# A fused LSH-attention and spatial-gating kernel: a wide hash product for the first pair, another order of the last batch's units, and per-batch priorities

## The chip, the cores and the metric

The kernel runs on one core of a Trainium2 chip. The metric is the device time of one execution in microseconds (us), lower is better. In the profile the engines are PE (TensorE's products), PEld (its weight loads), DVE (VectorE), ACT (ScalarE), POOL (GpSimd) and SP (SyncE, which issues all the transfers here).

## The reference, cut to what matters

Attention with 8 heads of width 64 over 4 batches of 768 rows, in which a query sees only the keys whose six sign bits (a hash by a random projection) are the same as its own; its output goes through a gated unit whose gate mixes rows with a 768 x 768 matrix.

```python
q_bits, k_bits = (q @ proj > 0), (k @ proj > 0)          # 6 bits per row
mask = bucket(q_bits)[:, :, :, None] == bucket(k_bits)[:, :, None, :]
attn = softmax(np.where(mask, q @ k.T / 8, -1e9))         # (4, 8, 768, 768)
x = (attn @ v).transpose(0, 2, 1, 3).reshape(4, 768, 512)
h = np.maximum(x @ w_in, 0.0)                             # 512 -> 1024
u, vv = h[..., :512], h[..., 512:]
v_n = (vv - mean) / np.sqrt(var + 1e-06)
v_s = np.einsum('ts,bsd->btd', w_spatial, v_n) + b_spatial[None, :, None]
out = (u * v_s) @ w_out                                   # 512 -> 512
```

## The kernel before, in words

Two heads make a pair, so there are 16 pairs, four per batch. For each pair (`pair`, L318) one load brings 128 x 2 x 768 numbers of k and q (L323). A hash product in float32 (L325) gives 4 x 32 rows; VectorE takes the sign (L331), ScalarE scales it (L333), and the rows go through DRAM (a write, L338, two reads, L342) into `hr`, where they stand as 12 rows of 64 per head among rows of zeros. ScalarE and VectorE split k and q into a high and a low half in float16 (`hl`, L354 and L357), and v likewise (`vp`, L361 and L363).

A pair has six row blocks. For each (`scores`), TensorE makes the scores of two heads in 16 products, three of the halves and one of the hash rows per half row and head; VectorE cuts them at a floor and takes the row maximum (L403, L406), ScalarE makes the exponentials and their sums (L411), VectorE the reciprocals (L413, L414), ScalarE the high half of the weights (L417), VectorE the low half (L419), and a transfer transposes both (L425). After three blocks a weighted product (`weighted`, 36 products in two column halves) makes half of the pair's `xt` (L446, L449).

When a batch's four pairs are done, `mlp` runs its 28 units on TensorE: six v (normalised by L479 to L515, POOL makes the low half, L518), then for each half of the rows four u, four s (L555, L558, L564, L567 make the gated block `g` in two halves) and three o. The units of one batch run beside the attention of the next batch; those of the last batch run alone. The gated unit's weights are loaded and converted once, in pieces (`weights` and `job`): 16 of w_in and 8 of w_out go through one step on ScalarE (L295), three on VectorE (L299 to L303) and a split (L242, L313), 12 of w_sp through two copies on ScalarE (L308, L309) and L313.

The order of all instructions is set when the program is built. Every step is given an engine, a duration, a key and its buffers (`op`); `plan` runs through time with these durations and, whenever an engine is free, gives it the ready step with the smallest key, if a buffer of its ring is free (6 for ex, 4 for pp, 2 for the score buffers, 1 for qk). The result is each engine's fixed order, and SP's too. A key is counted in row blocks: `g = NT*p + i` for block i of pair p, `k0 = NT*(p - 1) + 0.4` for a pair's preparation. The units have keys from `NT*NPAIR*(b + 1) + 2` on, and each step its offset, the same for all batches. For instance:

```python
op("PE", 1.36, g - 12.0, product, r=[hl, hrb], w=ps, kind="s")
op("DVE", 0.88, g, cut, r=[ps[e]], w=[ex[e], mx])
op("DVE", 0.93, g + 3.0, lambda e=e: nc.vector.scalar_tensor_tensor(
UNITS = [("v", i, 0) for i in range(NT)] + [x for h in range(2) for x in
         [("u", d, h) for d in range(NF)] + [("s", d, h) for d in range(NF)] + [("o", h * NT // 2 + i, 0) for i in range(NT // 2)]]
```

Of the kernel before, what the change touches and what calls it, by code (L numbers as in the profile page):

```python
# [34 lines left out]
def lsh_attention_spatial_gating(  # L35
# [34 lines left out]


# [8 lines left out]
    ws = [const.tile([P, NT, S], F16, name=f"ws{i}") for i in range(2)]  # L80
    wo = [const.tile([P, NF, DM], F16, name=f"wo{i}") for i in range(2)]
# [50 lines left out]

    def plan():


        SEM, MODE, DMA_LAT, SLOW = 0.1, 0.1, 1.3, 1.25
# [11 lines left out]
        fed = False  # L148
# [35 lines left out]
        while done < len(ops):  # L184
            nxt = None
            for e in free:
                while free[e] <= now:
# [24 lines left out]
                    if e == "PE":  # L212
                        if not fed:
                            d *= SLOW
                        fed = fed or o.kind == "m"
# [47 lines left out]
    Wv, Wu, Ws, Wo, Bt = Buf(), Buf(), Buf(), Buf(), Buf()  # L263

    def weights():
        vi, vo, vs = (x.rearrange("(c p) f -> p c f", p=P) for x in (w_in, w_out, w_sp))
        n = 0
        for src, dst, cs, lo, hi, m, f, W, key, dk in (
                (vi, wi, NPAIR, F2, DF, 256, SI, Wv, 5.0, 1.9), (vi, wi, NPAIR, 0, F2, 256, SI, Wu, 20.5, 1.0),
                (vs, ws, NT, 0, S, HS, SW, Ws, 28.0, 0.5), (vo, wo, NF, 0, DM, 256, SI, Wo, 33.5, 0.5)):  # L270
            for c in range(cs):
                for h in range(lo, hi, m):
                    job(n, src[:, c, h:h + m], [w[:, c, h:h + m] for w in dst], m, f, W, key)
                    n += 1
                    key += dk
        op("SP", 0.6, 27.0, lambda: nc.sync.dma_start(out=bt, in_=b_sp.partition_broadcast(P)), w=[Bt], land=1.0)

    def job(n, src, dst, m, f, W, key):
# [5 lines left out]
        op("SP", 0.6, key - 1.5, fetch, w=[raw], land=0.85 if m == 256 else 1.05)  # L284
        if src.dtype == F32:
            wb = raw
        else:
# [17 lines left out]
            for k, e, d in ((0, "ACT", 0.33), (1, "DVE", 0.2), (2, "DVE", 0.34), (3, "DVE", 0.34)):  # L305
                op(e, d, key - 12.0, lambda k=k: conv(k), r=[raw], w=[wb], lock=e == "DVE")
        if src.dtype == F32:
            op("ACT", 0.41, key, lambda: nc.scalar.activation(dst[0], wb.t[:, :m], AF.Copy, scale=f), r=[wb], w=[(W, n)])  # L308
            op("ACT", 0.41, key, lambda: nc.scalar.activation(wb.t[:, :m], wb.t[:, :m], AF.Copy, scale=f), w=[wb])  # L309
        else:  # L310
            op("ACT", 0.31, key + 1.5, lambda eng: cast(eng, dst[0], wb.t[:, :m]), r=[wb], w=[(W, n)], alt=("DVE", 0.2))
        op("POOL", 0.63 if m == 256 else 0.87, key,
           lambda: nc.gpsimd.tensor_tensor(out=dst[1], in0=wb.t[:, :m], in1=dst[0], op=ALU.subtract), r=[wb], w=[(W, n)], lock=True)  # L313
# [5 lines left out]
    def pair(p):  # L319
        b, r = divmod(p, NPAIR)  # L320
        k0 = NT * (p - 1) + 0.4 if p else -40.0
        qk, v32, hl, vp, hrb, hp, s0, s1 = (Buf(t) for t in ("qk", "v32", "hl", "vp", "hr", "m", "sg0", "sg1"))
        op("SP", 0.6, k0 - 1.9, lambda: nc.sync.dma_start(out=tile_of(qk, wk, [P, 2, S], F32, f"qk{p}"), in_=kq[b, r]), w=[qk], land=2.4)  # L323

        def hash_():  # L325
            t = tile_of(hp, ps_m, [P, 512], F32, f"hp{p}")
            matmuls([(t[32 * j:32 * j + 32, :HS], pj, qk.t[:, j // 2, (j % 2) * HS:(j % 2 + 1) * HS],
                      True, True, (0, 32 * j)) for j in range(4)])
# [11 lines left out]
        def rows(e):  # L340
            hrb.t = hr[p % NHR]
            nc.sync.dma_start(  # L342
                out=hrb.t[D * e:D * e + NR].rearrange("r g (c k) -> r (g c) k", c=2),
                in_=d.t.rearrange("(j r) k -> r j k", j=4)[16 * e:16 * e + NR])

        for e in range(2):
            op("SP", 0.6, k0 + 0.3 + 3.7, lambda e=e: rows(e), r=[d], w=[(hrb, e)], land=0.3)

        def part(g):
            return hl.t.rearrange("p (x g) s -> p x g s", g=2)[:, :, g]  # L350

        def high():
            tile_of(hl, wk, [P, 4, S], F16, f"hl{p}")
            nc.scalar.activation(part(0), qk.t, AF.Copy, scale=SQ)  # L354
# [19 lines left out]
    def scores(p, i, hl, hrb, pts):  # L374
# [22 lines left out]
        op("PE", 1.36, g - 12.0, product, r=[hl, hrb], w=ps, kind="s")  # L397

        for e in range(2):
# [5 lines left out]
            op("DVE", 0.88, g, cut, r=[ps[e]], w=[ex[e], mx])  # L405
        op("DVE", 0.08, g, lambda: nc.vector.tensor_scalar(tile_of(nb, wk, [P, 2], F32, f"nb{p}_{i}"), mx.t, -ISQ, None, op0=ALU.mult), r=[mx], w=[nb])  # L406
        for e in range(2):
# [4 lines left out]
            op("ACT", 0.92, g + 0.7, exp, r=[nb], w=[ex[e], sm])  # L412
        op("DVE", 0.08, g, lambda: nc.vector.tensor_scalar(tile_of(ri, wk, [P, 2], F32, f"ri{p}_{i}"), sm.t, 1e-9, 1.0 / SP, op0=ALU.add, op1=ALU.mult), r=[sm], w=[ri])  # L413
        op("DVE", 0.1, g, lambda: nc.vector.reciprocal(ri.t, ri.t), w=[ri])  # L414
        j = i % 3
        for e in range(2):
            op("ACT", 0.83, g - 0.7, lambda e=e: nc.scalar.activation(  # L417
                tile_of(pp[e], wk, [P, 2, 2, HS], F16, f"pp{p}_{i}_{e}")[:, 0], ex[e].t, AF.Copy, scale=ri.t[:, e:e + 1]), r=[ex[e], ri], w=[pp[e]])
            op("DVE", 0.93, g + 3.0, lambda e=e: nc.vector.scalar_tensor_tensor(  # L419
# [6 lines left out]
            op("SP", 1.5, g - 0.7, turn, r=[pp[e]], w=[(pts[e], j)], land=1.8)  # L426

    def weighted(p, h, vp, pts, xt):
# [10 lines left out]
        op("PE", 3.0, k - 0.7, product, r=[vp, *pts], w=[ps], kind="w")  # L439
# [3 lines left out]
        def hi():  # L443
            if h == 0:
# [3 lines left out]
        op("ACT", 0.37, k, hi, r=[ps], w=[(xt, h)])  # L448
        op("DVE", 0.47, k - 0.7, lambda: nc.vector.scalar_tensor_tensor(  # L449
# [5 lines left out]
    UNITS = [("v", i, 0) for i in range(NT)] + [x for h in range(2) for x in  # L455
             [("u", d, h) for d in range(NF)] + [("s", d, h) for d in range(NF)] + [("o", h * NT // 2 + i, 0) for i in range(NT // 2)]]

    def mlp(b):
        xt = [xts[b * NPAIR + r] for r in range(NPAIR)]
# [3 lines left out]
        vr, mv = {}, {}  # L463

        def v_unit(i, key):
# [22 lines left out]
            op("DVE", 0.1, key, aggr, r=[bs], w=[(m, i % 3)])  # L488
# [3 lines left out]
        def norm(g, key):  # L492
            m = mv[g]
            ve, r = Buf("ve"), Buf("rs")
            op("DVE", 0.1, key + 0.8, lambda: nc.vector.tensor_scalar(
                tile_of(ve, wk, [P, 3], F32, f"ve{b}_{g}"), m.t[:, :, 1], EPS_LN, None, op0=ALU.add), r=[m], w=[ve])
            op("ACT", 0.11, key, lambda: nc.scalar.activation(tile_of(r, wk, [P, 3], F32, f"rs{b}_{g}"), ve.t, AF.Ln), r=[ve], w=[r])
            op("ACT", 0.11, key, lambda: nc.scalar.activation(r.t, r.t, AF.Exp, scale=-0.5), w=[r])

            op("DVE", 0.08, key, lambda: nc.vector.tensor_mul(ve.t, ve.t, r.t), r=[r], w=[ve])  # L500
            op("DVE", 0.08, key, lambda: nc.vector.scalar_tensor_tensor(
                out=ve.t, in0=ve.t, scalar=-0.5 * SN, in1=r.t, op0=ALU.mult, op1=ALU.mult), r=[r], w=[ve])
            op("DVE", 0.08, key, lambda: nc.vector.scalar_tensor_tensor(
                out=r.t, in0=ve.t, scalar=1.5 * SN, in1=r.t, op0=ALU.add, op1=ALU.mult), r=[ve], w=[r])
            for j in range(3):
                i = 3 * g + j
                y = Buf("vy")
                op("DVE", 0.46, key - 3.4, lambda i=i, j=j, y=y: nc.vector.tensor_scalar(  # L508
# [8 lines left out]
                op("ACT", 0.51, key, hi, r=[y], w=[(x, i) for x in vn])  # L517
# [72 lines left out]
    for t in ("vn0", "vn1", "g0", "g1"):  # L590
        RING[t] = 1
# [64 lines left out]
```

## Time and profile before

| | |
|---|---|
| median of 3 runs | 668.69 us (668.39 to 670.16) |
| the profiled execution | 668.28 us, of which the span is 666.5 us |
| busy TensorE, VectorE, ScalarE, GpSimd | 584.6, 543.8, 495.7, 137.8 us |
| mean granted clock of TensorE | 0.931 |
| transfers' share of 16 engines' span | 82.6% |

The profile is of one execution. Its span runs from the first instruction's start to the last one's end; the device time holds 1.8 us more. Busy times are sums over an engine's instructions, and the granted clock is in parts of full speed: 1.00 is 2.4 GHz and the other level, 0.5, is 1.2 GHz, so that a mean between them is a mixture of the two.

### The profile page before, as it was taken

The page shows a single profiled execution, that of the slowest core. Times are in us where ns is not written, and L with a number is a line of the kernel's source. Part 1 is how long each engine was busy: PE and PEld are TensorE (multiplying, and loading weights), DVE is VectorE, ACT ScalarE, POOL GpSimd, SP SyncE. Part 2 cuts the span into 40 slices and gives each one's busy share as a digit, 9 for nine tenths or more (in the row PEclk, how much of TensorE's full clock was granted, in tenths as well). Part 3 has the DMA queues.
Part 4 walks back from the last instruction along what each step waited for, and adds up shares of the span by engine and source line. Part 5 has one row for each costly group of instructions (what it writes and reads, how often), then busy time and mean ns, then how long its engine had stood idle before and what let it go on. Part 6 is the DMA issues. An engine that isn't in the chain of part 4 may idle for free. (4 is left out here: it accounts for less than half of the span.)

```text
span 666.5 us, 12114 instructions
## 1 busy us (share of the span) xinstructions
PE 584.6 (88%) x4352; PEld 300.6 (45%) x4352; DVE 543.8 (82%) x1155; ACT 495.7 (74%) x879; POOL 137.8 (21%) x129
## 2 busy tenths in 40 slices
PE   2567666668989989999999999989999999999997
PEld 0223323333444445554445545544455555545453
DVE  3899988789999998899998988898999978834100
ACT  4678879889889778878879778778898787734111
POOL 2110022131122310140022410320124202204412
PEclk9656777776999999999999999999999999999999
DMA  6499999999967999989986989989898898860001
GB/s 239 146 206 219 202 216 214 203 193 208 205 136 154 206 203 222 206 167 198 229 177 122 216 157 232 157 180 221 159 187 166 150 185 143 146 131 1 17 32 47
DMA packets 318876, 113.28 MB, mean 170 GB/s; under 512 B 303328, under 2 KB 308448, under 8 KB 318816
## 3 DMA queue, kind: packets, MB, share of 16 engines
q1 hardware_dynamic: 318816, 112.51, 82.6%
q8 instruction: 34, 0.56, 0.3%
q14 instruction: 26, 0.21, 0.1%
HBM read 29.12 MB, written 7.86 MB: 55 GB/s over the span
## 5 line engine op out<-in xcount | busy, mean ns | idle before, releaser
L419 DVE SCALAR_TENSOR_TENSOR pp<-ex,ri,pp 128x768 f16<-128x768 f32 x192 | 204.5, 1080 | 24.5 <-ACT pp L417 24.2
L417 ACT ACTIVATE pp<-ex,ri 128x768 f16<-128x768 f32 x192 | 169.9, 926 | 54.3 <-issue 27.4
L255 PE MATMUL sp<-hl 64*128 64x384 f16 x1152 | 157.9, 357 | 47.2 <-DVE ex L403 46.8
L411 ACT ACTIVATE ex<-ex,nb 128x768 f32<-128x768 f32 x192 | 177.3, 924 | 16.3 <-DVE nb L406 16.0
L403 DVE TENSOR_SCALAR_CACHE_REDUCE ex<-sp 128x768 f32<-128x768 f32 x192 | 180.6, 946 | 9.1 <-PE sp L255 8.9
L255 PEld LDWEIGHTS <-hl 64*128 64x128 f16 x1152 | 63.6, 100 | 127.0 <-issue 96.5
L255 PE MATMUL pv<-pt,vp 128*64 128x384 f16 x1152 | 110.7, 344 | 6.1 <-DMA pt<-pp 6.1
L255 PE MATMUL sps<-ws,vn 128*128 128x384 f16 x576 | 98.1, 326 | 0.0
L255 PEld LDWEIGHTS <-vp 128*64 128x64 f16 x1152 | 72.2, 115 | 45.3 <-issue 16.4
L255 PE MATMUL sp<-hr 64*128 64x384 f16 x384 | 85.4, 358 | 0.0
L558 POOL TENSOR_TENSOR sy<-sy,u 128x384 f32<-128x384 f32 x32 | 42.8, 1338 | 165.7 <-DVE sy L555 156.2
L255 PEld LDWEIGHTS <-vn 128*128 128x128 f16 x576 | 54.7, 98 | 41.5 <-issue 7.0
L255 PE MATMUL ops<-wo,g 128*128 128x512 f16 x288 | 66.0, 380 | 2.0 <-POOL g L567 1.2
L255 PE MATMUL ups<-xt,wi 128*128 128x384 f16 x384 | 65.8, 326 | 0.0
L255 PE MATMUL vps<-wi,xt 128*128 128x512 f16 x288 | 65.3, 380 | 0.2 <-ACT xt L446 0.2
L518 POOL TENSOR_TENSOR vn<-vy,vn 128x512 f16<-128x512 f32 x24 | 29.3, 1233 | 155.7 <-ACT vn L515 155.7
L255 PEld LDWEIGHTS <-wi 128*128 128x128 f16 x384 | 36.2, 98 | 28.4 <-issue 5.4
L555 DVE SCALAR_TENSOR_TENSOR sy<-sps,bt 128x384 f32<-128x384 f32 x32 | 17.7, 552 | 37.1 <-PE sps L255 37.0
L255 PEld LDWEIGHTS <-g 128*128 128x128 f16 x288 | 26.6, 98 | 39.2 <-issue 4.1
L255 PEld LDWEIGHTS <-xt 128*128 128x128 f16 x288 | 27.0, 98 | 35.9 <-issue 4.4
L567 POOL TENSOR_TENSOR g<-sy,g 128x384 f16<-128x384 f32 x32 | 29.9, 934 | 44.9 <-ACT g L564 44.9
L255 PE MATMUL hp<-qk,hc 128*32 128x384 f32 x128 | 16.8, 603 | 22.7 <-DMA qk<-kq 22.7
(48 smaller groups left out, 490.2 us busy)
## 6 DMA issues: line engine op xcount, KB each, us to landing
qk<-kq SPq DMA_DIRECT2D x16, 768.0 KB
v<-v SPq DMA_DIRECT2D x16, 384.0 KB
out<-o SPq DMA_DIRECT2D x24, 256.0 KB
raw<-w_in SPq DMA_DIRECT2D x16, 256.0 KB
pt<-pp SPq DMA_TRANSPOSE x192
raw<-w_sp SPq DMA_DIRECT2D x12, 192.0 KB
raw<-w_out SPq DMA_DIRECT2D x8, 256.0 KB
dr<-sg SPq DMA_DIRECT2D x16, 96.0 KB
```

Of the source, the lines that this page charges most:

```text
L255: nc.tensor.matmul(out_, lhsT=lhsT, rhs=rhs, start=start, stop=stop, **({} if pos is None else {"tile_position": pos}))
L403: nc.vector.tensor_scalar(tile_of(ex[e], wk, [P, 2, HS], F32, f"ex{p}_{i}_{e}"), ps[e].t[:, :, :HS], -float(2 ** 27), None, op0=ALU.max, o ...
L411: nc.scalar.activation(ex[e].t, ex[e].t, AF.Exp, bias=nb.t[:, e:e + 1], scale=ISQ, accum_out=sm.t[:, e:e + 1])
L417: op("ACT", 0.83, g - 0.7, lambda e=e: nc.scalar.activation(tile_of(pp[e], wk, [P, 2, 2, HS], F16, f"pp{p}_{i}_{e}")[:, 0], ex[e].t, AF.Co ...
L419: op("DVE", 0.93, g + 3.0, lambda e=e: nc.vector.scalar_tensor_tensor(out=pp[e].t[:, 1], in0=ex[e].t, scalar=ri.t[:, e:e + 1], in1=pp[e].t ...
L518: op("POOL", 1.11, key - 6.0, lambda i=i, y=y: nc.gpsimd.tensor_tensor(out=vn[1].t[:, i], in0=y.t, in1=vn[0].t[:, i], op=ALU.subtract), r= ...
L555: op("DVE", 0.47, key, lambda: nc.vector.scalar_tensor_tensor(out=tile_of(y, wk, [P, HS], F32, f"sy{b}_{d}_{h}"), in0=ps.t[:, :HS], scalar ...
L558: op("POOL", 0.96, key - 6.0, lambda: nc.gpsimd.tensor_mul(y.t, y.t, u[h].t[:, d]), r=[(u[h], d)], w=[y], lock=True)
L567: op("POOL", 0.87, key, lambda: nc.gpsimd.tensor_tensor(out=gt[h][1].t[:, d], in0=y.t, in1=gt[h][0].t[:, d], op=ALU.subtract), r=[y], w=[( ...
```

## The change

Three things change. First, pair 0 has a preparation of its own (`first`): k and q are loaded in two transfers, the hash is a product with a 128 x 128 matrix `pj0` whose columns put each result on the row where `hr` wants it, and sign and scaling are made in place, in `hr`, without the way through DRAM. `pj0` and the shift `away` are made by eight small instructions of VectorE from the loaded constants. Second, in the last batch the six o units come last, and the second half's u, g0 and g1 lie in buffers of the rings of hl and vp. Third, nearly every step's key gets an offset per batch (`at`), and the planner's durations change a little: the product of scores from 1.36 to 1.31, TensorE slower by 1.3 until 150 us of planned time instead of 1.25 until the first unit, the landing of kq from 2.4 to 3.2 us. The weights' loads are keyed earlier and their conversions later; the weights' tiles of w_sp and w_out become four rings of one buffer.

```diff
+    pj0 = const.tile([P, P], F32, name="pj0")
+    nc.vector.memset(pj0, 0.0)
+    away = const.tile([P, 2], F32, name="away")
+    nc.vector.memset(away, 0.0)
+    for e in range(2):
+        n = slice(D * e, D * e + 2 * NB)
+        nc.vector.tensor_copy(away[n, e:e + 1], hv[n, 0:1])
+        nc.vector.tensor_scalar(away[n, 1 - e:2 - e], hv[n, 0:1], -1.0, 1.0, op0=ALU.mult, op1=ALU.add)
+        nc.vector.tensor_copy(pj0[D * e:D * e + D, n], hc[D * e:D * e + D, 16 * e:16 * e + 2 * NB])
...
+    def at(*by_batch):
+        return by_batch[batch[0]]
...
-        SEM, MODE, DMA_LAT, SLOW = 0.1, 0.1, 1.3, 1.25
+        SEM, MODE, DMA_LAT, SLOW, COLD = 0.1, 0.1, 1.3, 1.3, 150.0
...
-                (vi, wi, NPAIR, F2, DF, 256, SI, Wv, 5.0, 1.9), (vi, wi, NPAIR, 0, F2, 256, SI, Wu, 20.5, 1.0),
-                (vs, ws, NT, 0, S, HS, SW, Ws, 28.0, 0.5), (vo, wo, NF, 0, DM, 256, SI, Wo, 33.5, 0.5)):
+                (vi, None, NPAIR, F2, DF, 256, SI, Wv, 3.0, 1.1), (vi, None, NPAIR, 0, F2, 256, SI, Wu, 12.0, 0.5),
+                (vs, [P, NT, S], NT, 0, S, HS, SW, Ws, 28.0, 0.5), (vo, [P, NF, DM], NF, 0, DM, 256, SI, Wo, 33.5, 0.5)):
...
-        op("SP", 0.6, key - 1.5, fetch, w=[raw], land=0.85 if m == 256 else 1.05)
+        op("SP", 0.6, key - 1.5 - 20.8, fetch, w=[raw], land=0.85 if m == 256 else 1.05)
...
-                op(e, d, key - 12.0, lambda k=k: conv(k), r=[raw], w=[wb], lock=e == "DVE")
+                op(e, d, key + 18.4, lambda k=k: conv(k), r=[raw], w=[wb], lock=e == "DVE")
...
-            op("ACT", 0.41, key, lambda: nc.scalar.activation(dst[0], wb.t[:, :m], AF.Copy, scale=f), r=[wb], w=[(W, n)])
-            op("ACT", 0.41, key, lambda: nc.scalar.activation(wb.t[:, :m], wb.t[:, :m], AF.Copy, scale=f), w=[wb])
+            op("ACT", 0.41, key + 9.2, lambda: nc.scalar.activation(dst(0), wb.t[:, :m], AF.Copy, scale=f), r=[wb], w=[(W[0], n)])
+            op("ACT", 0.41, key - 37.3, lambda: nc.scalar.activation(wb.t[:, :m], wb.t[:, :m], AF.Copy, scale=f), w=[wb])
...
+        def first():
+            for g in range(2):
+                hp = Buf("sc")
+                def load(g=g):
+                    if g == 0:
+                        tile_of(qk, wk, [P, 2, S], F32, f"qk{p}")
+                    nc.sync.dma_start(out=qk.t[:, g], in_=kq[b, r][:, g])
+                def hash_(g=g, hp=hp):
+                    t = tile_of(hp, ps_sc, [P, 2, 512], F32, f"hp{p}_{g}")
+                    matmuls([(t[:, c, :HS], pj0, qk.t[:, g, c * HS:c * HS + HS], True, True, None) for c in range(2)])
+                def sign(g=g, hp=hp):
+                    nc.vector.tensor_scalar(hrb.t[:, g].rearrange("p (c k) -> p c k", c=2), hp.t[:, :, :HS], 0.0,
+                                            away[:, g:g + 1], op0=ALU.is_gt, op1=ALU.subtract)
...
+                op("SP", 0.6, k0 + g - 18.2, load, w=[(qk, g)], land=1.7)
+                op("PE", 1.35, k0 + g + 31.6, hash_, r=[(qk, g)], w=[hp], kind="hf")
+                op("DVE", 0.88, k0 + g + 5.1, sign, r=[hp], w=[(hrb, g)])
+                op("ACT", 0.74, k0 + g + 21.2, lambda g=g: nc.scalar.activation(hrb.t[:, g], hrb.t[:, g], AF.Copy, scale=(HQ, HK)[g]), w=[(hrb, g)])
...
-        op("PE", 0.8, k0 - 0.7, hash_, r=[qk], w=[hp], kind="h")
+            op("PE", 0.8, k0 + at(-2.2, -2.2, 28.8, 37), hash_, r=[qk], w=[hp], kind="h")
...
+        (later if p else first)()
...
-        op("PE", 1.36, g - 12.0, product, r=[hl, hrb], w=ps, kind="s")
+        op("PE", 1.31, g + at(-29.9, -30.6, -9, -1.4), product, r=[hl, hrb], w=ps, kind="s")
...
-            op("DVE", 0.88, g, cut, r=[ps[e]], w=[ex[e], mx])
+            op("DVE", 0.88, g + at(2.3, 1.5, 23.8, -15.4), cut, r=[ps[e]], w=[ex[e], mx])
...
-            op("ACT", 0.92, g + 0.7, exp, r=[nb], w=[ex[e], sm])
+            op("ACT", 0.92, g + at(1.9, 0.4, 37, -3.3), exp, r=[nb], w=[ex[e], sm])
...
-            op("DVE", 0.93, g + 3.0, lambda e=e: nc.vector.scalar_tensor_tensor(
+            op("DVE", 0.93, g + at(37.2, 33, 38.5, 34.4), lambda e=e: nc.vector.scalar_tensor_tensor(
...
-            op("SP", 1.5, g - 0.7, turn, r=[pp[e]], w=[(pts[e], j)], land=1.8)
+            op("SP", 1.5, g + at(4.7, 5.7, -12, -3.2), turn, r=[pp[e]], w=[(pts[e], j)], land=1.8)
...
+    def units(b):
+        v, u, s_, o = ([(x, i % m, i // m) for i in range(n)] for x, n, m in (("v", NT, NT), ("u", 2 * NF, NF), ("s", 2 * NF, NF), ("o", NT, NT)))
+        rest = s_[:NF] + o[:NT // 2] + u[NF:] + s_[NF:] + o[NT // 2:]
+        if b == B - 1:
+            rest = s_[:NF] + u[NF:] + s_[NF:] + o
+        return v + u[:NF] + rest
...
-                u[h] = Buf("u")
+                u[h] = Buf(("u", "hl")[late(h)])
...
-                gt[h] = [Buf("g0"), Buf("g1")]
+                gt[h] = [Buf("vp"), Buf("vp")] if late(h) else [Buf("g0"), Buf("g1")]
```

## Rows read from the trace of the kernel before

**Rows 1.** Stretches: from:to and length, busy us of PE, PEld, DVE, ACT, POOL; PEclk, DMA

```profile
0.00:21.10 21.10, 5.96 (x32) 1.54 (x32) 10.40 (x19) 9.74 (x15) 4.00 (x8) 1.00 0.63 211
21.10:100.00 78.90, 51.84 (x341) 22.80 (x342) 72.59 (x165) 60.44 (x109) 12.38 (x14) 0.65 0.93 203
100.00:140.00 40.00, 28.33 (x214) 15.31 (x215) 32.74 (x67) 36.19 (x66) 8.68 (x9) 0.74 0.96 206
140.00:165.38 25.38, 17.98 (x133) 8.70 (x129) 24.00 (x55) 22.46 (x42) 6.66 (x6) 0.66 0.97 201
165.38:250.00 84.62, 77.29 (x591) 39.03 (x590) 83.20 (x180) 69.85 (x129) 19.31 (x19) 1.00 0.90 182
250.00:595.55 345.55, 337.53 (x2690) 178.46 (x2688) 307.36 (x643) 278.43 (x486) 64.64 (x52) 1.00 0.94 181
595.55:666.50 70.95, 65.70 (x360) 34.74 (x360) 13.45 (x31) 18.57 (x37) 22.11 (x22) 1.00 0.06 23
```

**Rows 2.** Products by tile: ns min/median/max, first and last start in us

```profile
L255 PE MATMUL vps<-wi,xt x288: 379/379/390, 165.4 to 605.6; 128*128 128x512 f16 x144
L255 PE MATMUL sps<-ws,vn x576: 322/326/337, 217.1 to 653.6; 128*128 128x384 f16 x192
```

**Rows 3.** Timeline, 0 to 50 us: start, length, instruction [idle before it and releaser]

```profile
1.19 0.42 SPq L323 DMA_DIRECT2D qk<-kq  x1
...
5.88 1.48 ACT L354 ACTIVATE hl<-qk 128x1536 f16<-128x1536 f32 x1 [3.87 <-DMA qk<-kq]
...
8.85 0.33 SPq L338 DMA_DIRECT2D dr<-sg  x1
...
9.92 0.33 SPq L323 DMA_DIRECT2D qk<-kq  x1
...
10.54 0.37 SPq L342 DMA_DIRECT2D hr<-dr  x1
...
14.71 1.51 PE L255 MATMUL hp<-qk,hc 128*32 128x384 f32 x8 [7.21 <-DMA qk<-kq]
...
16.15 1.14 PE L255 MATMUL sp<-hl 64*128 64x384 f16 x6
...
21.10 0.95 DVE L403 TENSOR_SCALAR_CACHE_REDUCE ex<-sp 128x768 f32<-128x768 f32 x1
```

**Rows 4.** Groups of instructions: busy us, mean ns of one, idle before and its releasers

```profile
L403 DVE TENSOR_SCALAR_CACHE_REDUCE ex<-sp 128x768 f32<-128x768 f32 x192 | 180.6, 946 | 9.1 <-PE sp L255 8.9
L357 DVE SCALAR_TENSOR_TENSOR hl<-qk,hl 128x1536 f16<-128x1536 f32 x16 | 28.9, 1804 | 0.6 <-ACT hl L354 0.5
L255 PE MATMUL hp<-qk,hc 128*32 128x384 f32 x128 | 16.8, 603 | 22.7 <-DMA qk<-kq 22.7
L301 DVE SCALAR_TENSOR_TENSOR w<-raw,w 128x256 uint32<-128x256 uint32 x24 | 10.3, 437 | 0.1
```

**Rows 5.** Weight steps by tile: ns min/median/max, first and last start

```profile
L308 ACT ACTIVATE ws<-raw x12: 507/508/523, 92.0 to 147.5; 128x384 f16<-128x384 f32 x12
L309 ACT ACTIVATE raw<-raw x12: 506/522/524, 92.5 to 148.5; 128x384 f32<-128x384 f32 x12
...
L313 POOL TENSOR_TENSOR wi<-w,wi x16: 662/697/1620, 11.8 to 102.5; 128x256 f16<-128x256 f32 x16
```

**Rows 6.** TensorE's waits (us, times, longest): 165.4 to 595 us, then whole run

```profile
PE sp L255 <- DVE ex L403: 11.2, 19, 1.5
...
PE pv L255 <- DMA pt<-pp: 6.1, 7, 1.5
```

**Rows 7.** Timeline, 615 to 666.5 us

```profile
627.85 0.60 PE L255 MATMUL ops<-wo,g 128*128 128x512 f16 x2 [0.39 <-ACT g L564]
...
628.84 5.57 PE L255 MATMUL ops<-wo,g 128*128 128x512 f16 x25 [0.38 <-POOL g L567]
...
656.25 0.60 PE L255 MATMUL ops<-wo,g 128*128 128x512 f16 x2 [0.40 <-ACT g L564]
...
657.23 5.57 PE L255 MATMUL ops<-wo,g 128*128 128x512 f16 x25 [0.38 <-POOL g L567]
```

More of the change, by code (lines that the diff above doesn't have):

```diff
@@ L212, in plan @@
                     if e == "PE":
-                        if not fed:
+                        if now < COLD:
                             d *= SLOW
-                        fed = fed or o.kind == "m"
                         if kind[e] != o.kind:
@@ L320, in pair @@
         b, r = divmod(p, NPAIR)
+        batch[0] = b
         k0 = NT * (p - 1) + 0.4 if p else -40.0
         qk, v32, hl, vp, hrb, hp, s0, s1 = (Buf(t) for t in ("qk", "v32", "hl", "vp", "hr", "m", "sg0", "sg1"))
[L323 to L328, printed above, removed]
@@ L340, in rows @@
[L340 to L354, printed above, removed]
@@ new lines, in pair, with vhigh @@
+        (later if p else first)()
+        k1 = NT * p
+        def vhigh():
+            tile_of(vp, wk, [P, 2 * NT, 2 * D], F16, f"vp{p}")
+            nc.scalar.activation(vp.t[:, :, D:2 * D], v32.t, AF.Copy, scale=SQ)
+        op("SP", 0.6, k1 - 3.0 + at(-35.5, -10, -9.7, -22.7), lambda: nc.sync.dma_start(out=tile_of(v32, wk, [P, 2 * NT, D], F32, f"v32_{p}"), in_=v[b, r]), w=[v32], land=1.5)
+        op("ACT", 0.74, k1 + 0.5 + at(33.9, -0.9, 15.5, 39.3), vhigh, r=[v32], w=[vp])
+        op("DVE", 0.87, k1 + 0.6 + at(-7.9, -7.9, -1.5, 13.6), lambda: nc.vector.scalar_tensor_tensor(
@@ L437, in product @@
                      for c in range(NT) for n, (gv, gp) in enumerate(((1, 0), (0, 0), (1, 1))) for e in range(2)])
-        op("PE", 3.0, k - 0.7, product, r=[vp, *pts], w=[ps], kind="w")
+        op("PE", 2.95, k + at(11.2, 11.2, 13.6, 12.5), product, r=[vp, *pts], w=[ps], kind="w")
         f = SX / (SP * SQ)
@@ L463, in mlp, with late @@
         vr, mv = {}, {}
+        def late(h):
+            return b == B - 1 and h == 1
         def v_unit(i, key):
@@ L531, in product @@
                          for c in range(NPAIR) for n, (gw, gx) in enumerate(THREE)])
-            op("PE", 1.95, key - 3.0, product, r=[(x, h) for x in xt] + [Wu], w=[ps], kind="m")
+            op("PE", 1.95, key + at(39.7, 39.7, 7.9, 39), product, r=[(x, h) for x in xt] + [Wu], w=[ps], kind="m")
             def relu():
-                if d == 0:
+                if d == 0 and late(h):
+                    u[h].t = tile_of(u[h], wk, [P, 4, S], F16, f"u{b}_{h}").bitcast(F32)
+                elif d == 0:
                     tile_of(u[h], wk, [P, NF, HS], F32, f"u{b}_{h}")
                 nc.scalar.activation(u[h].t[:, d], ps.t[:, :HS], AF.Relu, scale=1.0 / SI)
-            op("ACT", 0.37, key, relu, r=[ps], w=[(u[h], d)])
+            op("ACT", 0.37, key + at(-30.3, -3.2, -2.9, -3.2), relu, r=[ps], w=[(u[h], d)])
         def s_unit(d, h, key):
             if h not in gt:
-                gt[h] = [Buf("g0"), Buf("g1")]
+                gt[h] = [Buf("vp"), Buf("vp")] if late(h) else [Buf("g0"), Buf("g1")]
             ps, y = Buf("m"), Buf("sy")
```

139 lines of the change are left out of this document (84 added, 55 removed).

## The prediction, made before the changed kernel was run

> **What bounds the kernel now.** I read the table of stretches first, then the waits inside them, then the first 50 and the last 50 us of the timeline. The run falls into five stages [rows 1]. Up to 21.1 us there is no cut of scores at all, and VectorE is busy for 10.4 us. From there to 165.38 us (batch 0's attention, with no gated unit to run beside it) VectorE works 72.59 + 32.74 + 24.00 = 129.3 of 144.3 us while TensorE works 98.2 at a granted clock of about two thirds: VectorE bounds. From 165.38, where the first v product starts [rows 2], to 250 us VectorE still works 83.20 of 84.62 and TensorE 77.29: VectorE bounds, narrowly. From 250 to 595.55 TensorE works 337.5 of 345.6 us and VectorE 307.4: TensorE bounds, at full clock. After 595.55 the last batch's products run alone, TensorE being nearly the whole chain.
>
> So an idle microsecond costs time on VectorE before 250 us and on TensorE after it. VectorE idles 10.7 us before 21.1, then 6.3, 7.3 and 1.4 (15.0 in all), then 1.4. TensorE idles 8.0 us between 250 and 595.55. These are all that a new order can win: 10.7 + 15.0 + 1.4 + 8.0, and the tail.
>
> **The first pair.** Before, the first hash waits for the whole 768 KB of pair 0; then comes a chain of sign, scaling, a write to DRAM and two reads back, and the first score product is also queued behind pair 1's hash, which waits for its own load until 14.71; products begin at 16.15, and the first cut is at 21.10 [rows 3]. The new path loads two halves, each followed by its own hash, sign and scaling; SP's queue loses the DRAM write and both reads and gains one load.
>
> Its time: the whole load takes 4.7 us from issue (1.19) to first use (5.88). The write at 8.85 let its first read go at 10.54, 1.7 us for a small transfer, so about 1.6 of the 4.7 is fixed, and I put the first half at 1.19 + 1.6 + 1.55 = 4.3 us, the second at 5.9. The wide hash of a half is two products over all 128 output rows. The eight narrow instructions of four products took 1.51 us together [rows 3] though one lasts 0.6 us on average [rows 4], so four ran side by side; wide ones cannot, and four instructions of a half cost between 0.75 us (half the narrow group) and 3.0 us (two per narrow group's time). I take 2.7, near the upper end, because the overlap of the narrow ones is in the rows. Hashes: 4.3 to 7.0 and 7.0 to 9.7. Sign over 768 elements read from PSUM: 0.95, as a cut [rows 4], to 10.7. Scaling: half of the 1.48 us row of hl, which has twice the elements [rows 3], 0.74, to 11.4. The first products then start at 11.5 and I let the cut follow 3 us behind, at 14.5 (before, 16.15 and 21.10), with pair 1's hash behind them: its load needs the buffer that the second hash frees at 9.7, against 9.92 before, so pair 1 is neither earlier nor later.
>
> The cut could thus start 6.6 us earlier, but VectorE bounds, and what counts is its idle time. Of its 10.40 us of work before 21.1 [rows 1], pair 1's part stays behind pair 1's load: 0.6 for the sign (half a cut's elements and a fixed part), 1.8 for hl [rows 4], 0.9 for vp (768 elements, as a cut). Two of the four weight blocks also come later, three steps of at most 0.44 each [rows 4], so about 2.3: 4.8 is left. New are eight set-up instructions, of 128 elements or fewer against 256 in the 0.44 us row, 0.13 each as I take it, 1.0 in all; and two signs of 0.95 for one of 0.6, 1.3. So VectorE is busy 7.1 us of the 14.5 and idles 7.4, against 10.7, for 2.3 of new work: that is 10.7 - 7.4 - 2.3 = 1.0 us; a third weight block drawn in would make it 2.2. I take **2 us**. The set-up waits for the small constant load and hides under the first half's; without that cover it costs its 1.0. Ends: a gain of 6.6 (the whole shift), a loss of 2.3.
>
> **The order in batch 0.** Of the 15.0 idle us, 7.3 lie at 100 to 140, where ScalarE works 36.19 of 40 [rows 1] and carries w_sp: 12 pairs of copies at 0.51 and 0.52, 12.4 us [rows 5], done from 92 to 148 us though the first spatial product starts only at 217 [rows 2]. The new offsets set the first copy behind every attention step of batch 0 on ScalarE (keys from 37, where batch 0's exponentials end near 25); between 165 and 250 ScalarE has 14.8 us free. I take 5 of the 7.3 and 1 of the other 7.7: **6 us**. w_in is all converted by 103 us [rows 5], 62 before the first v product; shifted later, its steps land where VectorE works 98% of the time at the latest, so I count nothing for them. The stretch from 165 to 250 gives 0. Ends: the 15.0 + 1.4 whole, or as much as the 7.3 more, if the moved copies stop ScalarE there as they do now.
>
> **The order after 250 us.** Of TensorE's waits since 165 those for VectorE's cuts are the most, 11.2 us [rows 6]. They end with a score buffer set free: they need an earlier cut. The new offsets differ by batch; the cuts move by -15 to +24, and the low-half step pp (L419), now +3, goes to +33 to +38, behind all else on VectorE. That favours cuts. Which sequence results is not in the rows; I take **2.5** of the 8.0, since the same VectorE work must pass and only its place changes. Ends: all 8.0, or as much lost. SP's queue gets no new kind of wait but a changed order; behind a transpose that waits there stand the next loads and transposes, so a low half made late is late for the weighted product.
>
> **The tail.** Twice TensorE empties after the last spatial unit of a half: it starts the output product, then waits for the scaled, gated and split block, 0.39 + 0.38 us at 627.85 and 628.84, and 0.40 + 0.38 at 656.25 and 657.23 [rows 7]. With all six output units last, the first gap is covered by four u units (48 products of three quarters of an output's width) and the second by three output units of the first half: 36 products at 5.57/25, 8 us for either, against some 3.5 from the last spatial product's end, two us before 627.85, to 628.84. Gain **1.5 us**, the four waits. The second half's u, g0 and g1 move into buffers of hl and vp, freed by 595.55, so nothing waits for a ring. If the cover failed, the same 1.5 remains: 0 gained.
>
> **Sum.** 2 + 6 + 2.5 + 1.5 = 12 us off the profiled execution's 668.28 us (its span is 666.5), 656.3; the median shown, 668.69, lies 0.4 above it, so 656.7, or 657.
>
> **Rivals.**
> *Only the fixed parts pay* (the new order packs no better): 2 + 1.5 = 3.5, 665. For it: VectorE works 98% at 165 to 250 and TensorE 98% after, so the rows leave little to pack. Against: the 7.3 idle us beside a full ScalarE have a named cause.
>
> *It does nothing measurable.* The earlier first pair only moves VectorE's idle time further back, because pair 1's load is no earlier: 1.5 us for the tail, 667. For: the load at 9.92 is unchanged by my own working. Against: weight blocks can fill the hole.
>
> *Slower: the low halves come too late.* With L419 last on VectorE, the transposes slip and weighted products wait in TensorE's order, with all score products behind them. Now there are seven such waits, 6.1 us, at most 1.5 each [rows 6]. If the 24 weighted products of batches 1 to 3 each waited 0.9 us (the mean of those seven), that is 21.6 less what of the 6.1 is there now, say 19, on the bound of that stage: 668.7 - 3.5 + 19 = 684. It decides from a mean wait of about 0.45 us over those 24, 11 us in all, which eats the 8.5 of reordering predicted and most of the fixed parts. For: the offset is among the largest in the change and every batch has it. Against: the rings of six ex and four pp buffers stop cuts from running far ahead, which forces L419 up.
>
> *Slower: the clock.* From 21 to 165 us the granted clock averages 0.65 to 0.74, and TensorE works about two thirds of the time [rows 1]; from 165 it is 1.00 without a break [rows 1]. If the new order broke TensorE's work at 165 to 250 so that a quarter of its 77.3 us ran at the lower level, that would cost 19 us less the 7.3 idle there, 12: no gain, about 669. The Trainium skill ("TensorE: Matmul & The Clock Gate", "HAM oscillation — how this bites in real kernels") has it that waits between bursts of products drop the clock to half, a rule against any reordering that puts waits there. By that rule, the trace agrees in batch 0 and shows no fall after 165.
>
> **Chances.** The forecast 0.60; only the fixed parts 0.20; nothing measurable 0.07; late low halves 0.09; the clock 0.04. A measurement of this kernel tells 0.3%, 2 us, from no change. The first two cases are faster, plus a little of the third's edge: 0.81. Within 0.3%: 0.09. Slower: 0.10, the late halves and the clock's upper part. The range must hold 8 in 10: its top, 667, takes in the fixed parts and the third case; its bottom, 645, lets the reordering give all of batch 0's 15 us and 4 after 250 with the tail and the start as taken (15 + 4 + 2 + 1.5, 646, and 1 for the spread of the runs). It leaves out the slower cases and the rare sum of all ends.
>
> **What would show it.** Right: first score product near 11.5 us and first cut near 14.5; w_sp's copies after 165; VectorE's idle time between 21 and the first v product near 9 us instead of 15; the first v product near 157 (8 earlier); TensorE's idle time after 250 near 5.5; no wait of an output product for g. Wrong, step by step: a hash half far from 2.7 us; a first v product still near 163; more or longer waits of weighted products for pt; a granted clock under 1.00 after the first v product; a gap before the last output units.

## The result, and the profile after

The changed kernel takes 650.58 us (median of 4 runs, 649.5 to 650.91) against 669.42 of the kernel before: a ratio of 0.9703, 95% interval 0.9658 to 0.9749, 18.8 us faster. The forecast was 657 in a range of 645 to 667. The profiled execution takes 650.47 us, with a span of 648.7, 17.8 less than before. One of the ten executions of e3 below, the one that was profiled, took 990.48 us at a mean granted clock of 0.558, the other nine 667.67 to 672.57 us at 0.923 to 0.944, so no stretch of e3 is used.

The stretches of the changed kernel, as in [rows 1] (busy us of PE, PEld, DVE, ACT, POOL, each with its count; granted clock, transfers):

```profile
0.00:250.00 250.00, 189.46 (x1381) 91.66 (x1382) 233.21 (x515) 203.81 (x364) 53.25 (x55) 0.89 0.97 203
250.00:560.00 310.00, 307.63 (x2477) 160.30 (x2477) 285.16 (x610) 262.87 (x460) 64.73 (x52) 1.00 0.95 186
560.00:648.70 88.70, 84.86 (x500) 44.88 (x496) 23.34 (x49) 28.11 (x52) 22.11 (x22) 1.00 0.23 54
```

The same cuts through the kernel before:

```profile
0.00:250.00 250.00, 181.40 (x1305) 87.38 (x1306) 222.94 (x482) 198.68 (x357) 51.02 (x55) 0.82 0.90 197
250.00:560.00 310.00, 301.98 (x2422) 159.15 (x2420) 282.83 (x595) 256.92 (x449) 56.34 (x45) 1.00 0.94 184
560.00:666.50 106.50, 101.25 (x629) 54.06 (x627) 37.98 (x81) 40.08 (x74) 30.41 (x30) 1.00 0.34 67
```

Where VectorE bounds, read how much work has passed; where TensorE bounds, read its idle time. A span is 250 us, plus TensorE's work that is left at 250 us, plus its idle time from there on, so the three parts add up by themselves. **By 250 us** 76 products more are done. TensorE is busy 584.63 us in all before and 581.96 after, so 403.2 and 392.5 us of its work are left: 10.7 us. **From 250 to 560** it idles 8.0 us before and 2.4 after: 5.6 us. **From 560 to the end** it idles 5.2 before and 3.8 after: 1.4 us. Together 17.7 of the 17.8.

The start, as in [rows 3]: the changed kernel's timeline, 0 to 26 us, with marked gaps.

```profile
1.18 0.42 SPq L353 DMA_DIRECT2D qk<-kq  x1
1.65 0.42 SPq L420 DMA_DIRECT2D v<-v  x1
2.12 0.91 SPq L301 DMA_DIRECT2D raw<-w_in  x2
...
3.07 0.43 SPq L295 DMA_DIRECT2D bt<-b_sp  x1
3.54 0.43 SPq L353 DMA_DIRECT2D qk<-kq  x1
...
4.59 2.90 PE L267 MATMUL hp<-qk,pj 128*128 128x384 f32 x4 [4.59 <-DMA qk<-kq]
...
9.85 2.93 PE L267 MATMUL hp<-qk,pj 128*128 128x384 f32 x4 [2.36 <-DMA qk<-kq]
...
11.03 0.83 ACT L366 ACTIVATE hl<-qk 128x768 f16<-128x768 f32 x1
...
12.06 0.94 DVE L373 SCALAR_TENSOR_TENSOR hl<-qk,hl 128x768 f16<-128x768 f32 x1
...
13.08 0.33 SPq L377 DMA_DIRECT2D qk<-kq  x1
...
17.23 0.96 DVE L462 TENSOR_SCALAR_CACHE_REDUCE ex<-sp 128x768 f32<-128x768 f32 x1 [0.15 <-PE sp L267]
```

The first cut comes at 17.23 instead of 21.10. The second half's load is not issued behind the first: four transfers stand between, and its hash starts at 9.85. Pair 1's load (L377) is issued at 13.08, against 9.92 before.

Batch 0's VectorE, two stretches of the changed kernel (before: 72.59 and 32.74, [rows 1]), then its copies of w_sp and its v products, as in [rows 5] and [rows 2]:

```profile
21.10:100.00 78.90, 52.53 (x369) 23.96 (x365) 77.86 (x175) 64.03 (x119) 17.48 (x17) 0.85 0.96 203
100.00:140.00 40.00, 24.45 (x188) 11.86 (x186) 34.38 (x72) 36.00 (x65) 6.85 (x7) 0.74 1.09 225
```

```profile
L327 ACT ACTIVATE ws<-raw x12: 505/507/510, 71.0 to 132.4; 128x384 f16<-128x384 f32 x12
...
L267 PE MATMUL vps<-wi,xt x288: 376/379/390, 158.1 to 589.9; 128*128 128x512 f16 x144
```

VectorE wins 5.3 us between 21 and 100 and only 1.6 between 100 and 140, where ScalarE is as full as before. Its waits for hashes and scores between 21.1 and 100 us, first the changed kernel's, then those before (us, times, longest):

```profile
DVE ex L462 <- PE sp L267: 0.6, 2, 0.4
```

```profile
DVE sg L331 <- PE hp L255: 3.0, 3, 1.8
DVE ex L403 <- PE sp L255: 2.6, 5, 0.8
```

TensorE's waits from 250 to 590 us in the changed kernel, for VectorE's cuts and for transposes:

```profile
PE sp L267 <- DVE ex L462: 1.4, 4, 0.5
PE pv L267 <- DMA pt<-pp: 0.5, 2, 0.3
```

The same two waits before, over the same 340 us:

```profile
PE sp L255 <- DVE ex L403: 5.0, 10, 1.0
PE pv L255 <- DMA pt<-pp: 2.7, 4, 1.1
```

Its products from 597.96 us on are one unbroken line where [rows 7] had four waits:

```profile
597.96 11.86 PE L267 MATMUL sps<-ws,vn 128*128 128x384 f16 x72
609.66 7.96 PE L267 MATMUL ups<-xt,wi 128*128 128x384 f16 x48
617.46 11.86 PE L267 MATMUL sps<-ws,vn 128*128 128x384 f16 x72
629.16 15.70 PE L267 MATMUL ops<-wo,g 128*128 128x512 f16 x72
```

### The profile page after: what moved, and what is told of

Same layout as the page of the kernel before. It is cut to its first block, busy times and chain, and to the rows that moved or that the text cites. A ratio compares the mean times of both kernels' runs of the same rounds, so it can differ in the third digit from the quotient of the medians.

```text
span 648.7 us, 12126 instructions
## 1 busy us (share of the span) xinstructions
PE 582.0 (90%) x4352; PEld 296.8 (46%) x4352; DVE 541.7 (84%) x1172; ACT 494.8 (76%) x874; POOL 140.1 (22%) x129
## 5 line engine op out<-in xcount | busy, mean ns | idle before, releaser
L478 DVE SCALAR_TENSOR_TENSOR pp<-ex,ri,pp 128x768 f16<-128x768 f32 x192 | 201.7, 1059 | 14.1 <-ACT pp L476 13.5
L476 ACT ACTIVATE pp<-ex,ri 128x768 f16<-128x768 f32 x192 | 173.3, 926 | 44.8 <-DVE ri L473 15.3
L267 PE MATMUL sp<-hl 64*128 64x384 f16 x1152 | 155.6, 355 | 45.8 <-DVE ex L462 45.0
L267 PEld LDWEIGHTS <-hl 64*128 64x128 f16 x1152 | 61.6, 100 | 125.4 <-issue 83.1
L267 PE MATMUL pv<-pt,vp 128*64 128x384 f16 x1152 | 107.8, 340 | 6.8 <-DMA pt<-pp 6.8
L267 PEld LDWEIGHTS <-vp 128*64 128x64 f16 x1152 | 67.9, 114 | 47.8 <-issue 16.3
L267 PE MATMUL sp<-hr 64*128 64x384 f16 x384 | 83.1, 356 | 0.3 <-ACT hr L371 0.3
L629 POOL TENSOR_TENSOR sy<-sy,u 128x384 f32<-128x384 f32 x32 | 37.2, 1162 | 158.3 <-DVE sy L626 79.8
L642 POOL TENSOR_TENSOR g<-sy,g 128x384 f16<-128x384 f32 x32 | 35.9, 1122 | 36.0 <-ACT g L639 36.0
L470 ACT ACTIVATION_READ_ACCUMULATOR ex<-ex,nb 128x1 f32 x192 | 36.2, 189 | 0.0
```

The lines of the kernel that those rows point to most:

```text
L267: nc.tensor.matmul(out_, lhsT=lhsT, rhs=rhs, start=start, stop=stop, **({} if pos is None else {"tile_position": pos}))
L470: nc.scalar.activation(ex[e].t, ex[e].t, AF.Exp, bias=nb.t[:, e:e + 1], scale=ISQ, accum_out=sm.t[:, e:e + 1])
L476: op("ACT", 0.83, g + at(0, -1, 0, 9.7), lambda e=e: nc.scalar.activation(tile_of(pp[e], wk, [P, 2, 2, HS], F16, f"pp{p}_{i}_{e}")[:, 0], ...
L478: op("DVE", 0.93, g + at(37.2, 33, 38.5, 34.4), lambda e=e: nc.vector.scalar_tensor_tensor(out=pp[e].t[:, 1], in0=ex[e].t, scalar=ri.t[:, ...
L629: op("POOL", 0.96, key + at(12, 24, 12, 30), lambda: nc.gpsimd.tensor_mul(y.t, y.t, u[h].t[:, d]), r=[(u[h], d)], w=[y], lock=True)
L642: op("POOL", 0.87, key + at(-40, -10.5, -40, -40), lambda: nc.gpsimd.tensor_tensor(out=gt[h][1].t[:, d], in0=y.t, in1=gt[h][0].t[:, d], op ...
```

## The experiments

Theory A is the prediction's sum. B lets one part carry through or each batch's offsets pay in their own stretch; C says the start only moves VectorE's idle time. After the first four runs two more theories were needed. L: the planner's result is one order among many, and any edit that makes it plan again gives another. R: the offsets make a good order whatever the lengths. Each ratio is to runs of the kernel before that stand beside it (medians 669.13 to 669.86 us).

**e1, structure only.** Every `at(...)` gets the one offset of before, and the weights' keys and the planner's constants go back:

```diff
-        op("PE", 1.31, g + at(-29.9, -30.6, -9, -1.4), product, r=[hl, hrb], w=ps, kind="s")
+        op("PE", 1.36, g + at(-12, -12, -12, -12), product, r=[hl, hrb], w=ps, kind="s")
```

> The changed kernel with the first pair's new path and the new last batch, but every offset, weight key and planner duration of before. Theory A (the prediction's terms): start 2 plus tail 1.5, so 3.5 us faster than before, ratio 0.995; the other 15 of the 19 us measured belong to the offsets. Theory B (the early start carries through a stage bound by VectorE and grows): at least half of the 19 us is here, ratio 0.986 or less.

675.72 us, ratio 1.0075 (1.004 to 1.011): a little slower than before. Neither theory expected this. Without new offsets the two structural parts do not pay at all in the order that the planner then makes.

**e2, the tail alone undone.**

```diff
-        if b == B - 1:
-            rest = s_[:NF] + u[NF:] + s_[NF:] + o
```

> The changed kernel with the last batch's units in the order of before. Theory A: the two waits before the output products come back, 0.4 + 0.4 us each, so 1.5 us slower than the changed kernel, ratio to before about 0.973. Theory B (the new order also lets the v and u units of the last batch start earlier): 3 us or more, and the products before the last weighted product stand in another order.

652.11 us, ratio 0.9726 (0.968 to 0.9772). That is 1.5 us above the changed kernel, but its runs (648.69 to 653.72) overlap with the changed kernel's, so the time alone does not show the part. Its timeline does, with the four waits again:

```profile
612.61 0.60 PE L267 MATMUL ops<-wo,g 128*128 128x512 f16 x2 [0.40 <-ACT g L637]
613.60 5.57 PE L267 MATMUL ops<-wo,g 128*128 128x512 f16 x25 [0.39 <-POOL g L640]
...
641.01 0.60 PE L267 MATMUL ops<-wo,g 128*128 128x512 f16 x2 [0.40 <-ACT g L637]
642.00 5.57 PE L267 MATMUL ops<-wo,g 128*128 128x512 f16 x25 [0.39 <-POOL g L640]
```

0.40 + 0.39 + 0.40 + 0.39 = 1.6. What stands ahead of the tail changes little (1388 products by 250 us, 4.6 us idle from 250 to 560 against 2.4), so the four waits can be read by themselves. Theory A holds for them.

**e3, the first pair's old path, planned again.**

```diff
-        (later if p else first)()
+        later()
```

> The changed kernel with pair 0 prepared as every other pair (hash rows through DRAM). Theory A: 2 us slower than the changed kernel (ratio to before about 0.973), the first cut late by 4 us. Theory B (the early start carries through): 4 us or more slower, ratio 0.977 or more. Theory C (VectorE only moves its idle time): no difference, 0.970.

668.93 us, ratio 1.0 (0.9976 to 1.0024): the whole gain is gone. By its number this is theory B (4 us or more). But 18 us is more than all the time before the first cut, which comes at 17.23 in the changed kernel and at 21.10 in the one before; this is what made theory L. The traces bear L out: aligned by line of the program, only 43% of VectorE's some 1170 instructions stand in the changed kernel's sequence, while e9, which keeps the order, has 99.9%.

**e4, new offsets in batch 0 only.**

```diff
-        op("PE", 1.31, g + at(-29.9, -30.6, -9, -1.4), product, r=[hl, hrb], w=ps, kind="s")
+        op("PE", 1.31, g + at(-29.9, -12, -12, -12), product, r=[hl, hrb], w=ps, kind="s")
```

> The changed kernel with the offsets of before in batches 1 to 3; batch 0, the weights' keys and the planner's durations stay new. Theory A (the prediction: two thirds of the order's gain is made in batch 0): of some 15 us, 10 stay, ratio about 0.978. Theory B (each batch's offsets work on their own batch, as the last cuts come 6, 12 and 20 us earlier by the end of batches 0, 1 and 2): 6 stay plus the fixed parts, ratio about 0.985.

669.67 us, ratio 1.0004 (0.9983 to 1.0025). Both theories fell. By 250 us 1346 products are done, 41 more than before, but TensorE then idles 12.0 us up to 560: the lead is won and lost.

**e5 to e8, the planner's durations drawn at random.** The work is the same; the planner sees other lengths and hands out another order.

```diff
+        draw = random.Random(1)
+        for o in ops:
+            f = 1.0 + 0.1 * draw.uniform(-1.0, 1.0)
+            o.on = {e: (d * f, x) for e, (d, x) in o.on.items()}
+            o.land *= 1.0 + 0.1 * draw.uniform(-1.0, 1.0)
```

> The changed kernel whose planner is given every step's duration times a random factor between 0.9 and 1.1 (a first draw); the work is the same, only the order that results differs. Theory L (the changed kernel's 651 is one lucky order, as e3 and e4 lost all of the gain with one part undone): 660 to 672 us, ratio 0.985 or more. Theory R (the offsets make a good order under many lengths): 648 to 656, ratio 0.98 or less.

> The same with a second draw of factors. Theory L: 660 to 672, and several us away from the first draw. Theory R: 648 to 656, within 3 us of the first draw.

> The kernel before with the same kind of factors on its planner's durations. Theory L: as wide a scatter as the changed kernel's, 664 to 680 us. Theory R (a property of the offsets): 668 to 674, and in any case 10 us or more above the changed kernel's draws.

> The kernel before with a second draw. Theories L and R as for the first draw; the four draws together tell how far two orders of one set of offsets lie apart.

The changed kernel's draws take 673.51 (ratio 1.0049, 1.0023 to 1.0076) and 675.21 us (1.01, 1.0061 to 1.014); those of the kernel before 695.63 (1.0385, 1.0338 to 1.0432) and 684.49 (1.0218, 1.0186 to 1.0249). All four lie above the ranges of theory L (660 to 672 and 664 to 680) and farther above those of theory R: another order loses the gain in both kernels, and more than expected. That e5 and e6 would lie several us apart did not come (1.7). What theory R expected besides, the draws of the kernel before 10 us or more above, came nearly: 9 to 22 us. But these two sets differ in the structural parts too, and e1, with the new structure and the old offsets, took 675.72, about what the draws with the new offsets take. So what the offsets give of this is not shown. The two stretches of e5:

```profile
0.00:250.00 250.00, 187.60 (x1380) 90.10 (x1382) 229.81 (x511) 202.04 (x361) 55.54 (x55) 0.84 0.93 201
250.00:560.00 310.00, 291.87 (x2313) 154.35 (x2308) 272.26 (x575) 247.51 (x431) 52.89 (x44) 0.99 0.89 179
```

and of e7:

```profile
0.00:250.00 250.00, 172.42 (x1245) 83.01 (x1246) 213.39 (x467) 189.53 (x339) 51.78 (x54) 0.82 0.88 191
250.00:560.00 310.00, 293.76 (x2296) 151.20 (x2296) 266.52 (x563) 244.81 (x425) 55.69 (x45) 0.97 0.88 175
```

e5 has the changed kernel's count of products at 250 us to one, though of another mix (397.3 us of TensorE's work are left, against 392.5), and then idles 18.1 us where the changed kernel idles 2.4. e7 lacks the lead (1245) and idles 16.2.

**e9, the second half's load right behind the first, the order otherwise kept.** The steps are planned as in the changed kernel; one is then moved by hand:

```diff
     order = plan()
+    loads = [o for o in order if o.fn.__name__ == "load"]
+    order.remove(loads[1])
+    order.insert(order.index(loads[0]) + 1, loads[1])
```

> The changed kernel in its own order, with one transfer moved: the second half of pair 0's load is issued right behind the first (near 1.7 us instead of 3.54). Theory A (the stage is bound by VectorE, whose idle time before the first cut shrinks): second half in use near 6.5 instead of 9.85, first cut near 14.5 instead of 17.2, 1 to 2.5 us faster than the changed kernel, ratio to before 0.968. Theory C (pair 1's load and the first weights arrive as before, so VectorE's idle time only moves): same as the changed kernel within 0.5 us, 0.971.

650.12 us, ratio 0.97 (0.9667 to 0.9732): the same as the changed kernel, the time of theory C. Its timeline:

```profile
4.55 4.83 PE L267 MATMUL hp<-qk,pj 128*128 128x384 f32 x8 [4.55 <-DMA qk<-kq]
...
11.00 0.83 ACT L366 ACTIVATE hl<-qk 128x768 f16<-128x768 f32 x1
...
12.04 0.94 DVE L373 SCALAR_TENSOR_TENSOR hl<-qk,hl 128x768 f16<-128x768 f32 x1
...
13.05 0.33 SPq L377 DMA_DIRECT2D qk<-kq  x1
...
17.40 0.96 DVE L462 TENSOR_SCALAR_CACHE_REDUCE ex<-sp 128x768 f32<-128x768 f32 x1 [0.16 <-PE sp L267]
```

The second hash is over at 9.4 instead of 12.8, but the second half's `hl` stands behind the first weight blocks in ScalarE's and VectorE's orders and still starts at 11.0; neither pair 1's load nor the cut moves. So the earlier cut on which theory A rests did not come about, and e9 does not decide between A and C.

**e10, the old path in the changed kernel's order.** Each step of pair 0's first half is replaced by the old path's, those of the second half by nothing; the three transfers through DRAM stand right behind the scaling:

```diff
+            mine = ops[-12:]
+            for o, fn in zip(mine, [whole, narrow, bits, through, both, rest] + [lambda: None] * 6):
+                o.fn = fn
```

> The changed kernel in its own order, but pair 0 goes the way of before (one load, narrow hash, rows through DRAM), each step at the place of the first half's step and the three DRAM transfers right behind the scaling. Theory A (the wide path itself is worth what the prediction gave it): 2 us slower than the changed kernel, ratio 0.974. Theory L (e3 lost 18 us only because the planner was run again and gave another order): nothing like 18 us is lost; between 2 us slower and 2 us faster than the changed kernel, 0.968 to 0.974. Theory E (the wide path is essential): 660 us or more.

653.04 us (650.5 to 656.06), ratio 0.9747 (0.971 to 0.9784); its profiled span is 649.1, with 1382 products by 250 us. Theory E fell, and with it the reading of e3 as the price of the old path. By the medians it is 2.5 us slower than the changed kernel, by the profiled executions 0.4, and the intervals overlap: A and L are not told apart. The old path's rows are read from `hr` at 13.8 us here, yet the first cut comes at 20.38, 3.2 us later than in the changed kernel, so a later start by itself cost little here:

```profile
10.19 0.33 SPq L429 DMA_DIRECT2D dr<-sg  x1
11.88 0.73 SPq L431 DMA_DIRECT2D hr<-dr  x2
13.80 0.10 PEld L267 LDWEIGHTS <-hr 64*128 64x128 f16 x1 [4.32 <-POOL wi L332]
...
20.38 0.95 DVE L496 TENSOR_SCALAR_CACHE_REDUCE ex<-sp 128x768 f32<-128x768 f32 x1
```

**e11, the offsets of before in batches 2 and 3.**

```diff
-        op("PE", 1.31, g + at(-29.9, -30.6, -9, -1.4), product, r=[hl, hrb], w=ps, kind="s")
+        op("PE", 1.31, g + at(-29.9, -30.6, -12, -12), product, r=[hl, hrb], w=ps, kind="s")
```

> The changed kernel with the offsets of before in batches 2 and 3; the planner makes the same order as the changed kernel's until batch 2's steps come in. Theory B (each batch's offsets pay in their own stretch): at 250 us as many products done as in the changed kernel, then TensorE idle again for some 8 us until the tail instead of 2.4, so 656 to 658, ratio 0.982. Theory L (a lead is lost when the order behind it is not the one chosen with it, as e4 lost batch 0's): 663 or more, 0.99.

672.61 us, ratio 1.0041 (1.0017 to 1.0064): theory L.

```profile
0.00:250.00 250.00, 188.80 (x1385) 92.15 (x1386) 234.06 (x516) 205.59 (x366) 53.94 (x55) 0.84 0.97 204
250.00:560.00 310.00, 291.87 (x2322) 151.78 (x2322) 275.38 (x585) 251.74 (x436) 52.60 (x44) 0.98 0.90 180
```

The first 250 us are the changed kernel's (1385 products); then TensorE idles 18.1 us. Hardly anything earlier differs, so the whole difference of the spans, 672.4 against 648.7, is the price of the order behind 250 us: 15.7 us more idle up to 560, 2.0 more after it, and 6.0 more of busy time, about what a granted clock of 0.98 in place of 1.00 makes over 310 us (4% of them at half speed). The waits from 250 to 560 us are those of the prediction, for a score buffer that a cut sets free (1.4 us in the changed kernel) and for transposes. Behind such a wait the clock falls, as two stretches show:

```profile
PE sp L267 <- DVE ex L462: 11.8, 10, 2.2
PE pv L267 <- DMA pt<-pp: 2.7, 4, 1.2
```

```profile
353.00:355.00 2.00, 0.32 (x1) 0.09 (x1) 2.00 (x6) 0.90 (x2) 0.00 (x0) 1.00 0.84 227
355.00:357.00 2.00, 1.54 (x10) 0.83 (x11) 1.89 (x9) 1.37 (x3) 0.00 (x0) 0.54 1.00 197
```

**e12, the draw of e5, a tenth as wide.**

```diff
+            f = 1.0 + 0.01 * draw.uniform(-1.0, 1.0)
```

> The changed kernel with random factors between 0.99 and 1.01 on the planner's durations. Theory L (the order is one choice among many that lie 10 to 25 us above it): 658 to 675 us even with so small a shift. Theory R' (the order is kept under small shifts and lost only under the 10% of e5 and e6): 650 to 654.

677.59 us, ratio 1.0102 (1.0056 to 1.0148), with 1334 products by 250 us and 14.8 us idle up to 560. One per cent is enough: R' fell, and the time lies above L's range (658 to 675) too.

## Why the prediction was right, point by point

The direction holds and the time lies in the range. The gain of 12 us was too small by a third (18.8 measured), and several of its reasons do not hold. That the sum came so near is in part luck: its terms price idle time and not a particular order, and e1, e4, e5, e6, e11 and e12, for which it would have named a gain too, gained nothing.

*The first pair* (2 us). The wide hash took 2.90 and 2.93 us a half, for 2.7. Until 21.1 us VectorE works 14.2 us (11.53 until 17.23 and 2.65 after) for 10.40; of the 3.8 more, some 2.3 are new work, as the prediction had it, so 1.5 of old work comes earlier. The step that failed is the second half's load "at 5.9": `op` makes every step depend on the first user of its buffer, so by the planner's code the second load waits until the first has landed. Its hash began at 9.85, the first score product at 13.07 and the cut at 17.23, not 14.5. By e9 the late load itself cost nothing in this order. "Pair 1 is neither earlier nor later" failed too: the buffer was not freed by the second hash but by the last `hl` on VectorE, which ends at 13.0 and lets pair 1's load go at 13.08, 3.2 us later than before, where `hl` ends at 9.84 and the load goes at 9.92; in e9 the hash is over at 9.4 and the load still goes at 13.05, behind `hl`. By e10 the wide path by itself is worth some 0 to 2.5 us. One reading was a mixture: the "0.6 us on average" of a narrow product holds both levels of the clock, and those of the first 20 us last 0.85; four side by side remain the likely reading.

*Batch 0's order* (6 us, with the start 8). The lead at 250 us is 10.7 us for 8: near in size, but the place is not right. The copies of w_sp did not go behind 165; they came earlier (71 to 132 us), and between 100 and 140 ScalarE is full as before and VectorE idles 5.6 us, for 7.3. The step that failed read "keys from 37" as "late": by the code of `plan` a key only ranks the steps that are ready, and an engine with nothing better takes the largest key at once. The gain came between 21 and 100 us, where VectorE's waits for hashes and scores shrank from 5.6 to 0.6 us and its idle time from 6.3 to 1.0. Which of the new offsets did that is open.

*The order after 250 us* (2.5 us) was mis-sized: 5.6 of the 8.0 idle us went. The prediction took a part "since the same VectorE work must pass". What the runs show in its place is that this stretch depends on the very order (products, work and idle time are of the one profiled execution of each; what the clock costs is in the work):

| | products by 250 us | TensorE's work left at 250 us | TensorE idle, 250 to 560 us | median, us |
|---|---|---|---|---|
| before | 1305 | 403.2 | 8.0 | 669.4 |
| changed | 1381 | 392.5 | 2.4 | 650.6 |
| e1, e4 | 1285, 1346 | 407.7, 400.8 | 11.5, 12.0 | 675.7, 669.7 |
| e11 | 1385 | 398.5 | 18.1 | 672.6 |
| new offsets, drawn: e5, e6, e12 | 1380, 1299, 1334 | 397.3, 404.0, 406.0 | 18.1, 14.2, 14.8 | 673.5, 675.2, 677.6 |
| old offsets, drawn: e7, e8 | 1245, 1273 | 418.4, 411.4 | 16.2, 14.8 | 695.6, 684.5 |

Eight orders planned anew idle 11.5 to 18.1 us there, the kernel before 8.0, the changed one 2.4. Both kernels are single orders that lie well below what their offsets give under other lengths.

*The tail* (1.5 us) holds to a tenth: the four waits are gone, and they are back in e2 with 1.6 us.

*The rivals.* "Only the fixed parts pay" and "nothing measurable" fell; the structure alone, under an order of its own, is slower (e1). The late low halves did not come: weighted products waited 1.5 us for transposes after 158 us, three times, though L478 has the last place on VectorE. The clock's fall, a sign of being wrong, came but was short: the first v product starts at 158.1, the clock is 0.66 from 170 to 175 us, and from 180 us on it stays at full. In e11 it costs some 6 us.

What the offsets are worth apart from the choice is not shown: three drawn orders with the new ones (e5, e6, e12) average 675.4 us and two with the old 690.1. They idle alike from 250 to 560 us (15.7 and 15.5 us) and differ in the lead at 250 (1338 products on average against 1259). Five draws are few, and the two sets differ in the first pair's path and the last batch's order as well (e1). Draws of the new structure with the old offsets would tell; they were not made. Which of the 46 offsets do it stays open: every edit of one makes the planner give another order, and the order by itself moves the time by up to 27 us (e12).

## What to carry to other kernels

When a planner writes the order, undoing a part and planning again measures the new order together with the part: keep the order and swap the step (e9, e10), or draw several orders for each variant. In a run that changes its bound, count work done where one engine bounds and idle time where the other does; a lead is only kept if what follows keeps the bounding engine fed. A static order that keeps its bounding engine 98% busy is worth choosing among many, and worth choosing again after every edit.

## What was not expected of the hardware

One order planned with durations up to one per cent off costs 27 us of 651 on the chip, though the work is the same but for a few weight splits that go to VectorE instead of ScalarE (e12).

And the granted clock of a profile can be wrong at its start. From 20 to 50 us the record of the changed kernel says 1.00 and that of the kernel before 0.54, yet the score products of those 30 us last the same, 0.52 us, and those from 200 us on, at 1.00 in both, 0.32. First the changed kernel's stretch and products, then those before:

```profile
20.00:50.00 30.00, 20.04 (x108) 7.70 (x104) 28.80 (x66) 22.67 (x44) 6.63 (x6) 1.00 0.75 175
...
L267 PE MATMUL sp<-hl x72: 472/524/524, 20.3 to 49.6; 64*128 64x384 f16 x72
```

```profile
20.00:50.00 30.00, 18.75 (x101) 7.74 (x103) 26.35 (x64) 21.72 (x41) 6.12 (x7) 0.54 0.78 189
...
L255 PE MATMUL sp<-hl x60: 474/524/524, 24.8 to 47.4; 64*128 64x384 f16 x60
```

So the higher means of the changed kernel's early stretches (0.85 against 0.65 from 21 to 100 us) are in part the record's and say nothing of the gain. Whether the lower level costs time while VectorE bounds is open.
